# Blocks of w1 and w2 prepared in the f steps instead of in the second product, and the last group of the first product's output taken in another order

## Chip, core and metric

The kernel runs on one core of one Trainium2 chip. The metric is the device time of one execution in microseconds (us). Three runs of the kernel before lie between 1381.03 and 1382.69 us, with a median of 1381.96 us.

## The reference

Attention in two steps feeds two gated products one after the other. All inputs are float32 (the weights arrive as 64-bit words and are converted in the kernel).

```python
p_packed = sm_attn(p, k, v)              # 8 batches, 8 heads, 32 packed queries, head size 64
out = sm_attn(q, p_packed, p_packed)     # 576 tokens per batch
x = out as (4608 tokens, 512)
# first MoE
g = x @ w_gate;  val = x @ w_val         # 512 -> 1536
x = (silu(g) * val) @ w_out              # 1536 -> 512
# second MoE
a = x @ w1;  b = x @ w2                  # 512 -> 1024
h = a * b @ w3                           # 1024 -> 1024
return h @ w_out2                        # 1024 -> 512
```

## The kernel before

Every float32 product is made of three TensorE matmuls: each operand is split into a high part (a cast on ScalarE) and a low part (a subtraction on VectorE or GpSimd), and high times high, high times low and low times high are summed in PSUM. In tile names the last letter tells the part: `uh` and `ul`, `woh` and `wol`, `w3h` and `w3l`.

Engines are PE (TensorE), DVE (VectorE), ACT (ScalarE), POOL (GpSimd) and SP (SyncE, which issues the DMAs). Each engine runs its own instructions in order. The order in the f steps is set when the program is built, by a scheduler with its own estimates, so an edit in one place can move instructions in another. In stage 5 the order is that of the code.

After the attention the first MoE runs in four passes P = 0 to 3, of two batches (1152 tokens) each. A pass has twelve f steps, one for each 128 columns of w_gate and w_val:

- `c_mm` and `c_out`: the packed attention times the weights gives PSUM tile `pc`; ACT makes `ch` of it, DVE `cl`.
- `stage1`: for each of the two batches, twelve matmuls into `pg`, twelve into `pv`. ACT puts the silu of `pg` into `u`, DVE multiplies `u` by `pv`, ACT makes `uh`, POOL `ul`.
- `stage3`: each three f steps make a group. In the first f step after it, six tiles `px` (j = 0 to 5) of 18 matmuls each (three f values, n = 0 to 2, times three parts, times two halves) take up the group; ACT or DVE adds a tile to its accumulator `acc`. The last group, of f = 9, 10, 11 of pass 3, has no f step after it and runs at the end.

`pc`, `pg`, `pv`, `px` and `pw` share four PSUM tiles: a new one starts only when what reads the old one in its place is done.

In passes 1 and 2 there is room beside the f steps, and blocks of w1 and w2 are converted there (`w12_conv`): a block is loaded as 64-bit words into a `raw` tile, a shift on DVE (`vx`), an activation on ACT and a merge on DVE make float32 of it, and it goes to DRAM (`w12d`). In pass 3 the product w3 times w_out2 is made beside the f steps (`w3_task`): w3 is converted (`vx_w`, `vt_w`), transposed on DVE (`w3T`, one buffer), split by ACT and POOL (`w3h`, `w3l`), multiplied into `pw`, and DVE or ACT writes `w3o`, for the second half (`c` = 1) by adding `pw` to `part`, which is the first half's result read back from DRAM.

Stage 5 makes a and b of the second MoE with seven products in place of eight, on sums of 256-wide blocks of w1, w2 and of x. For each of six groups g of tokens and eight steps f it runs seven products of six matmuls (`pA`, `pB`, `pC`). The seven weight blocks of a step are the tiles `ws`. Group g = 0 makes them: `load_w12` reads w12d back, `ws_sums` makes four sums on DVE, `ws_block` splits each of the seven and stores them to DRAM (`wsd`). Groups 1 to 5 load them from there (`ws_load`). Stage 7 (`po`) multiplies a times b with the product of w3 and w_out2 and writes the output.

Of the kernel before, what the change touches and what calls it, by code (L numbers as in the profile page):

```python
# [38 lines left out]
def packed_attention_moe_kernel(  # L39
# [255 lines left out]
    def raw_src(key):  # L295
        what, *at = key.split("_")
        at = [int(x) for x in at]
        if what == "wo2":
            c, kk = divmod(at[0], NH)
            return w_out2[512 * c:512 * c + 512, :].rearrange("(i k a) n -> k i a n", k=NH, a=32)[kk]  # L300
        if what == "w3":
            c, r = at
            return w3[128 * r:128 * r + 128, 512 * c:512 * c + 512].rearrange(
                "(b rr) (i n) -> i b rr n", rr=4, i=4)
        if what == "w":
            return (w_gate, w_val)[at[1]][:, 128 * at[0]:128 * at[0] + 128].rearrange(
                "(k p) n -> p k n", p=128)
        if what == "wo":
            return w_out[128 * at[0]:128 * at[0] + 128, :]
        x, c, h = w12_list[at[0]]  # L310
        return (w1, w2)[x][128 * c:128 * c + 128, 512 * h:512 * h + 512]

    raw_at = [0]
    load_after = {}
# [2 lines left out]
    def raw_load():  # L317
        if raw_at[0] < len(raw_q):
            key = raw_q[raw_at[0]]
            src = raw_src(key)  # L320
            raw_at[0] += 1
            blocks = src.shape[0] == 4
            t = vc.tile([128, 512] if blocks else [128] + list(src.shape[1:]), I64, tag="raw",
                        name=f"raw_{key}", bufs=5)
            if blocks:
# [5 lines left out]
            raw_t.append((key, t))  # L331

    def conv(key, t):

# [322 lines left out]

    CW = 2 * S // 3

    def stage3(P, g, e):  # L660
        for j in range(ND // 2 * 3 // 2 * e, ND // 2 * 3 // 2 * (e + 1)):
            t = psum(f"px{P}_{g}_{j}")
            for n in range(GF):
                f = GF * g + n
                uh, ul = (x.rearrange("p b a s -> p (b a s)") for x in u_pair[P, f])
                wh, wl = wo_t[P, f]
                for w, x, first, last in (
                    (wh, uh, n == 0, False), (wh, ul, False, False), (wl, uh, False, n == GF - 1),
                ):
                    for h in range(2):  # L670
                        d, c = divmod(2 * j + h, 3)
                        nc.tensor.matmul(  # L672
                            t[:, h, 0:CW], lhsT=w[:, 128 * d:128 * d + 128], rhs=x[:, CW * c:CW * c + CW],
                            start=first, stop=last,
                        )
            if g == 0:
                o = up.tile([128, 2, CW], F32, tag=f"acc{j}", name=f"acc{P}_{j}", bufs=1)
                nc.scalar.copy(o, t[:, :, 0:CW])
                acc[j] = o
            else:  # L680
                o = acc[j]
                nc.vector.tensor_tensor(out=o, in0=o, in1=t[:, :, 0:CW], op=ALU.add)  # L682
            if g == NG - 1:
                for h in range(2):
                    d, c = divmod(2 * j + h, 3)
                    t0 = 2 * S * P + CW * c
                    if j % 3 == 1:
                        nc.sync.dma_start(X2d[d, :, t0:t0 + CW], o[:, h])
                    elif h == 0:
                        nc.sync.dma_start(X2d[d, :, t0:t0 + 2 * CW], o.rearrange("p h s -> p (h s)"))  # L690


    def w12_conv(i):
        x, c, h = w12_list[i]
        t = vl.tile([128, 512], F32, tag="vu", name=f"w12t{i}")
        conv(f"w12_{i}", t)
        nc.sync.dma_start(
            w12d[4 * h:4 * h + 4, :, x, c, :].rearrange("f p n -> p f n"),
            t.rearrange("p (f n) -> p f n", n=128))


    wo2_t, w3T = {}, {}
# [42 lines left out]
    def w3_step(new, old):  # L745
        if old is not None:
            w3_mm(old)
        if new is not None:
# [8 lines left out]
    x2_t, x2r_t, w12r_t, wsrc, ws_t, wg_at = {}, {}, {}, {}, {}, []  # L757

    def load_w12(f):
        t = xp.tile([128, 2, 2, 256], F32, tag="wf", name=f"w12r{f}")  # L760
        nc.sync.dma_start(t.rearrange("p x k n -> p x (k n)"), w12d[f].rearrange("p x c n -> p x (c n)"))
        w12r_t[f] = t

    def ws_sums(f):
        t = w12r_t.pop(f)
        a11, a12, a21, a22 = (t[:, x, kh] for x in range(2) for kh in range(2))
        sa = vl.tile([128, 2, 256], F32, tag="vu", name=f"wsa{f}")
        sb = vl.tile([128, 2, 256], F32, tag="vu", name=f"wsb{f}")
        tt = nc.vector.tensor_tensor
        tt(out=sa[:, 0], in0=a21, in1=a22, op=ALU.add)  # L770
        tt(out=sa[:, 1], in0=sa[:, 0], in1=a11, op=ALU.subtract)
        tt(out=sb[:, 0], in0=a11, in1=a21, op=ALU.subtract)
        tt(out=sb[:, 1], in0=a12, in1=sa[:, 1], op=ALU.subtract)
        wsrc[f] = {"A11": a11, "A12": a12, "A22": a22, "S1": sa[:, 0], "S2": sa[:, 1],
                   "S3": sb[:, 0], "S4": sb[:, 1]}

    def ws_tile(g, f, k):
        if f == 0:
# [78 lines left out]
    for n, (P, f) in enumerate(steps):  # L857
# [39 lines left out]
        if P == 0:  # L897
# [2 lines left out]
            wo_split(P, f)  # L900
            if n >= 2:
                pin.clear()
        i = n - NF - 3
        if 0 <= i < len(w12_list):
            pin.update(pin_at)
            w12_conv(i)
            pin.clear()
        if P + 1 < NPR:
            q_tasks(2 * P + 2, 0, f)
            q_tasks(2 * P + 3, 5, f)  # L910
        if pend is not None:
            stage3(*pend, 1)
            pend = None
        C_t.pop((P, f))
        if f % GF == GF - 1:
            pend = (P, f // GF)
        if P == NPR - 1:
# [13 lines left out]
                x2_prep(0, 2)  # L931
            if f == 11:
                x2_prep(0, 3)
                load_w12(0)
                ws_sums(0)
                for k in range(7):
                    ws_block(0, k)
    for e in range(2):
        stage3(*pend, e)
        if e == 0:  # L940
            load_w12(1)
            ws_sums(1)
            load_w12(2)
    up.release()
    aB.release()
    wop.release()
# [24 lines left out]
    def stage5(g, f):  # L971
# [3 lines left out]
        def product(k, first):  # L975
            n, _, name = PROD[k]
            xh, xl = x2_t[g, name]
            w = ws_t[f, k]
            for d in range(2):
                for i, (hl, r) in enumerate(((0, xh), (0, xl), (1, xh))):  # L980
                    nc.tensor.matmul(bk[n], lhsT=w[:, hl, 128 * d:128 * d + 128], rhs=r[:, d],  # L981
                                     start=(first and d == 0 and i == 0), stop=(d == 1 and i == 2),
                                     skip_group_check=not first)

        def ahead(k):

            if g == 0 and f + 1 < NF2:
                ws_block(f + 1, k)
            n = (NF2 - 1) * g + f + 1
            ng, nf = divmod(n, NF2 - 1)  # L990
            if f and 0 < ng < NG2:
                ws_load(ng, nf + 1, k)

        def keep(name, t):
# [113 lines left out]
```

## Time and profile before

| | before |
|---|---|
| median of 3 runs | 1381.96 us |
| profiled execution | 1378.52 us |
| its span, first to last instruction | 1376.7 us |
| mean granted TensorE clock in it | 0.995 |
| PE busy | 1344.1 us (98%) |
| DVE busy | 658.7 us (48%) |
| ACT busy | 572.3 us (42%) |
| POOL busy | 386.0 us (28%) |
| DMA queue, share of its 16 engines' span | 53.8%, 228.64 MB |

The profile is of one execution, 3.4 us shorter than the median run; 1.8 us of that execution lie outside the span. Busy matmuls are counted from start to modelled end, so time in which TensorE runs at the lower clock counts as busy too.

### The profile page before, as it was taken

The page shows a single profiled execution, that of the slowest core. Times are in us where ns is not written, and L with a number is a line of the kernel's source. Part 1 is how long each engine was busy: PE and PEld are TensorE (multiplying, and loading weights), DVE is VectorE, ACT ScalarE, POOL GpSimd, SP SyncE. Part 2 cuts the span into 40 slices and gives each one's busy share as a digit, 9 for nine tenths or more (in the row PEclk, how much of TensorE's full clock was granted, in tenths as well). Part 3 has the DMA queues.
Part 4 walks back from the last instruction along what each step waited for, and adds up shares of the span by engine and source line. Part 5 has one row for each costly group of instructions (what it writes and reads, how often), then busy time and mean ns, then how long its engine had stood idle before and what let it go on. Part 6 is the DMA issues. An engine that isn't in the chain of part 4 may idle for free.

```text
span 1376.7 us, 25585 instructions
## 1 busy us (share of the span) xinstructions
PE 1344.1 (98%) x10196; PEld 1235.3 (90%) x10196; DVE 658.7 (48%) x962; ACT 572.3 (42%) x956; POOL 386.0 (28%) x309
## 2 busy tenths in 40 slices
PE   6889999999999999999999999999999999999998
PEld 4669899999999999999898989989899899898997
DVE  2875867346563466462354378733413333234230
ACT  4784644235432444344544136433323233233231
POOL 0323322323322233253443226502112022021120
PEclk9999999999999999999999999999999999999999
DMA  9997766534455444145343238928548367285441
GB/s 281 314 268 212 228 188 200 153 97 133 125 127 181 124 135 123 55 144 148 120 130 104 82 121 308 347 70 254 173 131 254 105 198 231 74 253 170 132 152 46
DMA packets 195335, 230.28 MB, mean 167 GB/s; under 512 B 71056, under 2 KB 128400, under 8 KB 195216
## 3 DMA queue, kind: packets, MB, share of 16 engines
q1 hardware_dynamic: 195216, 228.64, 53.8%
q8 instruction: 81, 1.33, 0.4%
q14 instruction: 38, 0.31, 0.1%
HBM read 179.04 MB, written 49.55 MB: 166 GB/s over the span
## 4 chain that ended last, share of the span: by engine, by line
PE 85%; POOL 1%; DVE 1%; ACT 1%; issue 0%; DVEq 0%; POOLq 0%; ACTq 0%
PE px L672 20%; PE pA L981 15%; PE po L1045 14%; PE pg L441 10%; PE pv L441 9%; PE pB L981 7%; PE pC L981 4%; PE pc L409 3%; PE pw L736 3%; PE psq L206 1%; POOL wo2l L89 0%; POOL ul L89 0%; DVE u L450 0%; DVE xB21l L89 0%; ACT vt_wo L346 0%
## 5 line engine op out<-in xcount | busy, mean ns | idle before, releaser
L89 POOL TENSOR_TENSOR ul<-u,uh 128x576 fp32r<-128x576 f32 x96 | 146.7, 1528 | 329.3 <-ACT uh L93 324.2
L1001 POOL TENSOR_TENSOR c<-s,s 128x384 f32<-128x384 f32 x48 | 49.2, 1024 | 375.7 <-ACT s L996 375.5
L672 PE MATMUL px<-uh,woh 128*128 128x384 f32 x576 | 148.0, 337 | 2.4 <-DVE acc L682 1.4
L672 PE MATMUL px<-ul,woh 128*128 128x384 f32 x576 | 147.8, 337 | 2.5 <-POOL ul L89 2.5
L672 PE MATMUL px<-uh,wol 128*128 128x384 f32 x576 | 147.2, 336 | 0.0
L996 ACT COPY s<-pA 128x384 f32<-128x384 f32 x144 | 69.2, 481 | 182.6 <-PE pA L981 181.2
L450 DVE TENSOR_TENSOR u<-u,pv 128x576 f32<-128x576 f32 x96 | 71.8, 749 | 108.1 <-PE pv L441 98.2
L93 ACT CAST uh<-u 128x576 fp32r<-128x576 f32 x96 | 64.6, 673 | 115.1 <-DVE u L450 114.8
L682 DVE TENSOR_TENSOR acc<-acc,px 128x768 f32<-128x768 f32 x72 | 68.1, 948 | 92.4 <-PE px L672 92.2
L1045 PE MATMUL po<-wo_hi,abl 128*128 128x512 f32 x288 | 112.2, 390 | 0.0
L1045 PE MATMUL po<-wo_lo,abh 128*128 128x512 f32 x288 | 112.2, 389 | 0.0
L1045 PE MATMUL po<-wo_hi,abh 128*128 128x512 f32 x288 | 112.0, 389 | 0.0
L672 PEld LDWEIGHTS px<-uh,woh 128*128 128x128 f32 x576 | 103.5, 189 | 5.3 <-DVE acc L682 1.9
L672 PEld LDWEIGHTS px<-ul,woh 128*128 128x128 f32 x576 | 104.8, 189 | 3.1 <-POOL ul L89 3.1
L672 PEld LDWEIGHTS px<-uh,wol 128*128 128x128 f32 x576 | 104.9, 189 | 0.0
L89 DVE TENSOR_TENSOR abl<-ab,abh 128x768 fp32r<-128x768 f32 x48 | 48.6, 1013 | 105.1 <-ACT abh L93 105.1
L89 POOL TENSOR_TENSOR wol<-wof,woh 128x512 fp32r<-128x512 f32 x48 | 63.2, 1330 | 108.2 <-ACT woh L93 105.5
L441 PE MATMUL pg<-aTh,ch 128*128 128x288 f32 x384 | 87.2, 308 | 2.1 <-ACT u L446 1.2
L446 ACT ACTIVATE u<-pg 128x576 f32<-128x576 f32 x96 | 62.5, 651 | 60.6 <-PE pg L441 59.1
L441 PE MATMUL pv<-aTh,ch 128*128 128x288 f32 x384 | 82.9, 297 | 0.9 <-DVE cl L89 0.6
L441 PE MATMUL pg<-aTh,cl 128*128 128x288 f32 x384 | 82.3, 296 | 0.0
L441 PE MATMUL pv<-aTh,cl 128*128 128x288 f32 x384 | 82.2, 295 | 0.0
(309 smaller groups left out, 3099.0 us busy)
## 6 DMA issues: line engine op xcount, KB each, us to landing
ws<-wsd SPq DMA_DIRECT2D x245, 256.0 KB, 3.1
wf<-Wd SPq DMA_DIRECT2D x36, 512.0 KB, 4.8
wsd<-ws SPq DMA_DIRECT2D x49, 256.0 KB, 3.1
wof<-wod SPq DMA_DIRECT2D x36, 256.0 KB, 3.0
x2r<-X2d SPq DMA_DIRECT2D x24, 384.0 KB, 4.7
out_dram<-o SPq DMA_DIRECT2D x36, 256.0 KB, 2.0
km<-in_k_dram SPq DMA_DIRECT2D x16, 512.0 KB, 6.9
vm<-in_v_dram SPq DMA_DIRECT2D x16, 512.0 KB, 7.9
```

The source lines that it names most:

```text
L89: return eng.tensor_tensor(out=out, in0=src, in1=hi.bitcast(F32), op=ALU.subtract)
L93: nc.scalar.copy(hi, src)
L409: nc.tensor.matmul(t[hs[at], b, Q], lhsT=PTd[es, 2 * (2 * P + b) + Q, hs[hq]], rhs=w[es, 2 * Q + hq // 2].rearrange("p g n -> p (g n)"), s ...
L441: nc.tensor.matmul(t[:, hf, 0:HS], lhsT=w[:, b % 2, Q, cols], rhs=x[:, Q, hf, :], start=first, stop=last,)
L446: x = nc.scalar.activation(u, t[:, :, 0:HS], AF.Silu)
L450: x = nc.vector.tensor_tensor(out=u, in0=u, in1=t[:, :, 0:HS], op=ALU.mult)
L672: nc.tensor.matmul(t[:, h, 0:CW], lhsT=w[:, 128 * d:128 * d + 128], rhs=x[:, CW * c:CW * c + CW], start=first, stop=last,)
L682: nc.vector.tensor_tensor(out=o, in0=o, in1=t[:, :, 0:CW], op=ALU.add)
L981: nc.tensor.matmul(bk[n], lhsT=w[:, hl, 128 * d:128 * d + 128], rhs=r[:, d], start=(first and d == 0 and i == 0), stop=(d == 1 and i == 2) ...
L996: nc.scalar.copy(o, t)
L1001: on.tensor_tensor(out=r, in0=o, in1=t, op=op)
L1045: nc.tensor.matmul(t, lhsT=a[:, j, cols], rhs=w[:, f], start=first, stop=last)
```

## The change

- A block is now a pair (f, d): the four 128x128 pieces that step f of stage 5 needs from 128 rows of both halves of w1 and w2. They are loaded by four DMAs into one raw tile.
- Blocks are converted two at a time in every third f step of passes 1 and 2 (the steps that also run `stage3`), eight steps with two blocks each. There the four sums are made (DVE), all seven pieces are split (ACT with DVE, and ACT with POOL) and stored to `wsd`. `w12d`, `load_w12`, `ws_sums` and `ws_block` go.
- Group 0 of stage 5 loads its `ws` from `wsd` as the others do. A block in `wsd` has another layout: a load takes pieces of 1 KB where it took 2 KB.
- Raw loads are filled up to five in flight, or two while blocks of w1, w2 or w_out2 are next; before, each conversion issued one load.
- The last `px` group: for tiles 0 to 3 the matmuls of n = 0 and 1 (f = 9 and 10) come first, then n = 2 tile by tile.

The core of the diff:

```diff
-    w12_list = [(x, c, h) for h in range(2) for x in range(2) for c in range(ND)]
+    w12_list = [(f, d) for f in range(NF2) for d in range(2)]
...
+    def raw_fill():
+        if w12_at[0] == len(w12_list):
+            depth = 5
+        else:
+            depth = 2 if raw_q[raw_at[0]].startswith(("w12", "wo2")) else 5
+        while raw_at[0] < len(raw_q) and len(raw_t) < depth:
+            raw_load()
...
-        if not in_front[0]:
-            raw_load()
+        if not in_front[0] and not key.startswith("w12"):
+            raw_fill()
...
+    def stage3_last(P, g):
+        ahead = {j: psum(f"px{P}_{g}_{j}") for j in range(4)}
+        for j in ahead:
+            stage3_mm(P, g, j, ahead[j], range(GF - 1))
+        for j in range(ND // 2 * 3):
+            t = ahead.get(j) or psum(f"px{P}_{g}_{j}")
+            stage3_mm(P, g, j, t, range(GF - 1 if j in ahead else 0, GF))
+            stage3_out(P, g, j, t)
...
+    def w12_blocks(i):
+        f, d = w12_list[i]
+        t = w12_t.pop(i).rearrange("p (k n) -> p k n", k=4)
+        a11, a12, a22, a21 = (t[:, k] for k in range(4))
+        x = vc.tile([128, 512], I32, tag="vx", name=f"w12s{i}").bitcast(F32).rearrange("p (k n) -> p k n", k=4)
+        s1, s2, s3, s4 = (x[:, k] for k in range(4))
+        tt = nc.vector.tensor_tensor
+        tt(out=s1, in0=a21, in1=a22, op=ALU.add)
+        tt(out=s2, in0=s1, in1=a11, op=ALU.subtract)
+        tt(out=s3, in0=a11, in1=a21, op=ALU.subtract)
+        tt(out=s4, in0=a12, in1=s2, op=ALU.subtract)
+        for src, k0, k1, on in ((t[:, 0:3], 0, 3, "dve"), (x, 3, 7, "pool")):
+            o = vc.tile([128, k1 - k0, 2, 128], F32R, tag="raw", name=f"w12p{i}_{k0}", bufs=5)
+            split(o[:, :, 0], o[:, :, 1], src, sub_on=on)
+            w12_out.append((wsd[f, d, :, k0:k1], o))
+        w12_at[0] += 1
...
     def ws_load(g, f, k):
         t = ws_tile(g, f, k)
-        nc.sync.dma_start(t.bitcast(F32).rearrange("p h (d n) -> p h d n", d=2), wsd[f, k])
+        nc.sync.dma_start(t.bitcast(F32), wsd[f, :, :, WSK[k]].rearrange("d p h n -> p d (h n)"))
...
-        i = n - NF - 3
-        if 0 <= i < len(w12_list):
+        w12_new = range(2 * (n - NF) // 3, 2 * (n - NF) // 3 + 2) if 0 < P < NPR - 1 and f % GF == 0 else ()
+        if w12_new:
             pin.update(pin_at)
-            w12_conv(i)
+            for i in w12_new:
+                w12_conv(i)
             pin.clear()
+            for i in w12_new:
+                w12_blocks(i)
...
-                load_w12(0)
-                ws_sums(0)
                 for k in range(7):
-                    ws_block(0, k)
-    for e in range(2):
-        stage3(*pend, e)
-        if e == 0:
-            load_w12(1)
-            ws_sums(1)
-            load_w12(2)
+                    ws_load(0, 0, k)
+    stage3_last(*pend)
...
-            if g == 0 and f + 1 < NF2:
-                ws_block(f + 1, k)
             n = (NF2 - 1) * g + f + 1
             ng, nf = divmod(n, NF2 - 1)
-            if f and 0 < ng < NG2:
+            if (f or g == 0) and ng < NG2:
                 ws_load(ng, nf + 1, k)
```

The matmuls are the same before and after. The change moves instructions on the in-order engines, and three places show it. In these rows the number behind a name and an underscore is a batch in pairs, an f, a tile or a buffer: `u_8` is the u of f = 8, `px_3_1` tile 1 of group 3, `w3o_0` the first output of the second half of w3, `w_1_6` the seventh block of that half.

First, VectorE in pass 3, f = 7 to 8. Before:

```order
573 L450 TENSOR_TENSOR u_7_8474<-u_7_8474,pv_7_8489 128x576
574 L450 TENSOR_TENSOR u_7_8527<-u_7_8527,pv_7_8542 128x576
575 L742 TENSOR_TENSOR w3o_0_8573<-part_8559,pw_1_0_8558 128x512
576 L719 STREAM_TRANSPOSE w3T(1, 3)_8737<-vt_w_1_3_8678 128x512
577 L350 SCALAR_TENSOR_TENSOR vt_w_1_5_8776<-vt_w_1_5_8776,vx_w_1_5_8777 128x512
578 L347 TENSOR_SCALAR vx_w_1_7_8951<-raw_w_1_7_8683 128x512
579 L89 TENSOR_TENSOR cl_9_8614<-pc_9_8596,ch_9_8613 128x1024
580 L450 TENSOR_TENSOR u_8_8617<-u_8_8617,pv_8_8632 128x576
581 L742 TENSOR_TENSOR w3o_1_8669<-part_8655,pw_1_1_8654 128x512
582 L719 STREAM_TRANSPOSE w3T(1, 4)_8770<-vt_w_1_4_8743 128x512
```

Now, from the w3T(1, 4) of the same f step on (L771 is the transpose, L794 the write of w3o):

```order
656 L771 STREAM_TRANSPOSE w3T(1, 4)_9009<-vt_w_1_4_8982 128x512
657 L364 SCALAR_TENSOR_TENSOR vt_w_1_5_9015<-vt_w_1_5_9015,vx_w_1_5_9016 128x512
658 L464 TENSOR_TENSOR u_8_8927<-u_8_8927,pv_8_8942 128x576
659 L771 STREAM_TRANSPOSE w3T(1, 5)_9094<-vt_w_1_5_9015 128x512
660 L361 TENSOR_SCALAR vx_w_1_6_9101<-raw_w_1_6_8766 128x512
661 L364 SCALAR_TENSOR_TENSOR vt_w_1_6_9100<-vt_w_1_6_9100,vx_w_1_6_9101 128x512
662 L794 TENSOR_TENSOR w3o_0_8817<-part_8803,pw_1_0_8802 128x512
663 L771 STREAM_TRANSPOSE w3T(1, 6)_9183<-vt_w_1_6_9100 128x512
664 L89 TENSOR_TENSOR cl_10_9038<-pc_10_9020,ch_10_9037 128x1024
665 L361 TENSOR_SCALAR vx_w_1_7_9190<-raw_w_1_7_8831 128x512
666 L364 SCALAR_TENSOR_TENSOR vt_w_1_7_9189<-vt_w_1_7_9189,vx_w_1_7_9190 128x512
667 L464 TENSOR_TENSOR u_9_9041<-u_9_9041,pv_9_9056 128x576
```

w3o_0 stood right behind the second u of f = 7 and ahead of w3T(1, 3); it now stands behind w3T(1, 5) and the merge of vt_w_1_6. w3o_1 to w3o_3, which before were spread over f = 8, now come behind the u of f = 9. TensorE's order here is unchanged: pw_1_0, pc_9, the pg and pv of f = 8 with pw_1_1 and pw_1_2 between them, pw_1_3, pc_10, pg and pv of f = 9, pw_1_4, px_2_0. In the built program pw_1_0 to pw_1_3 lie in the four PSUM tiles, pc_10 waits for w3o_0, pg_9 for cl_10, pv_9 for the silu on ACT, pw_1_4 for u_9; each follows the other in one PSUM tile.

The DMA queue of SyncE at the same place, now (before, the loads of raw_w_1_7 stood ahead of the store of w3o_0, L743):

```order
297 L332 DMA raw_w_1_6_8766<-in_moe_w_dram 32x4x128 x4
298 L783 DMA part_8803<-wo3d 128x512
299 L332 DMA raw_w_1_7_8831<-in_moe_w_dram 32x4x128 x2
300 L795 DMA wo3d<-w3o_0_8817 128x512
301 L332 DMA raw_w_1_7_8831<-in_moe_w_dram 32x4x128 x2
302 L388 DMA wf_11_8894<-Wd 128x1024
303 L403 DMA wof_9_8896<-wod 128x512
```

Two of the four loads of raw_w_1_7 now stand behind the store of w3o_0, and on ACT the conversion of w_1_7 stands ahead of the silu of f = 9.

Second, TensorE in the last px group. Before, the first tile is finished before the second begins:

```order
2355 L672 MATMUL px_3_0_9322<-uh_9_8831,woh_9_8748 128x384 x2
2356 L672 MATMUL px_3_0_9322<-ul_9_8832,woh_9_8748 128x384 x2
2357 L672 MATMUL px_3_0_9322<-uh_9_8831,wol_9_8749 128x384 x2
2358 L672 MATMUL px_3_0_9322<-uh_10_9153,woh_10_9099 128x384 x2
2359 L672 MATMUL px_3_0_9322<-ul_10_9154,woh_10_9099 128x384 x2
2360 L672 MATMUL px_3_0_9322<-uh_10_9153,wol_10_9100 128x384 x2
2361 L672 MATMUL px_3_0_9322<-uh_11_9247,woh_11_9214 128x384 x2
2362 L672 MATMUL px_3_0_9322<-ul_11_9248,woh_11_9214 128x384 x2
2363 L672 MATMUL px_3_0_9322<-uh_11_9247,wol_11_9215 128x384 x2
```

Now, at the end of the matmuls that do not need f = 11:

```order
2378 L684 MATMUL px_3_3_9549<-ul_9_9071,woh_9_8987 128x384 x2
2379 L684 MATMUL px_3_3_9549<-uh_9_9070,wol_9_8988 128x384 x2
2380 L684 MATMUL px_3_3_9549<-uh_10_9392,woh_10_9338 128x384 x2
2381 L684 MATMUL px_3_3_9549<-ul_10_9393,woh_10_9338 128x384 x2
2382 L684 MATMUL px_3_3_9549<-uh_10_9392,wol_10_9339 128x384 x2
2383 L684 MATMUL px_3_0_9546<-uh_11_9486,woh_11_9453 128x384 x2
2384 L684 MATMUL px_3_0_9546<-ul_11_9487,woh_11_9453 128x384 x2
```

The first matmul that reads uh_11 was the 13th of the group and is now the 49th.

Third, VectorE in pass 0, f = 2, where q of the next batch is transposed in two instructions for the product psq. Before:

```order
160 L157 STREAM_TRANSPOSE qT_0_1836<-qr_0_1762 128x576
161 L450 TENSOR_TENSOR u_2_1869<-u_2_1869,pv_2_1884 128x576
162 L157 STREAM_TRANSPOSE qT_0_1836<-qr_0_1762 128x576
163 L350 SCALAR_TENSOR_TENSOR wf_4_1903<-wf_4_1903,vx_w_1_1910 128x4x128
164 L347 TENSOR_SCALAR vx_wo_1949<-raw_wo_1755 128x512
165 L450 TENSOR_TENSOR u_2_1917<-u_2_1917,pv_2_1932 128x576
166 L350 SCALAR_TENSOR_TENSOR wof_2_1948<-wof_2_1948,vx_wo_1949 128x512
```

Now:

```order
160 L464 TENSOR_TENSOR u_2_1870<-u_2_1870,pv_2_1885 128x576
161 L364 SCALAR_TENSOR_TENSOR wf_4_1904<-wf_4_1904,vx_w_1_1911 128x4x128
162 L156 STREAM_TRANSPOSE qT_0_1837<-qr_0_1763 128x576
163 L361 TENSOR_SCALAR vx_wo_1950<-raw_wo_1718 128x512
164 L364 SCALAR_TENSOR_TENSOR wof_2_1949<-wof_2_1949,vx_wo_1950 128x512
165 L156 STREAM_TRANSPOSE qT_0_1837<-qr_0_1763 128x576
166 L464 TENSOR_TENSOR u_2_1918<-u_2_1918,pv_2_1933 128x576
```

The second transpose now stands behind the shift and the merge of a block of w_out.

## Rows read from the trace of the kernel before

**Rows 1.** The page, first part: busy time of each engine.
```profile
PE 1344.1 (98%) x10196; PEld 1235.3 (90%) x10196; DVE 658.7 (48%) x962; ACT 572.3 (42%) x956; POOL 386.0 (28%) x309
```
**Rows 2.** Waits of PE: total us, times, longest us.
```profile
PE px L672 <- POOL ul L89: 2.5, 2, 1.5
PE px L672 <- DVE acc L682: 1.4, 1, 1.4
PE px L672 <- ACT uh L93: 1.0, 2, 0.7
```
**Rows 3.** Chain of waits, pass 3: start us, us, what.
```profile
636.32 9.37 PE px L672 x54
```
**Rows 4.** Timeline of PE, last px group: start, us, what, idle before.
```profile
799.88 0.51 PE L672 MATMUL px<-uh,woh 128*128 128x384 f32 x2
...
807.51 0.84 PE L672 MATMUL px<-uh,wol 128*128 128x384 f32 x2
808.15 0.84 PE L672 MATMUL px<-uh,woh 128*128 128x384 f32 x2
...
825.50 0.34 PE L981 MATMUL pA<-xB11h,ws 128*128 128x384 f32 x1
```
**Rows 5.** Windows there: busy PE, PEld, DVE, ACT, POOL; PEclk; DMA.
```profile
805.00:810.00 5.00, 3.53 (x10) 3.13 (x11) 4.52 (x4) 0.00 (x0) 1.98 (x1) 0.51 0.24 71
```
**Rows 6.** Timeline of POOL, last px group.
```profile
802.89 4.09 POOL L89 TENSOR_TENSOR ul<-u,uh 128x576 fp32r<-128x576 f32 x2 [4.00 <-ACT uh L93]
```
**Rows 7.** Timeline of DVE, pass 3, f = 7 to 9.
```profile
732.64 0.69 DVE L742 TENSOR_TENSOR w3o<-part,pw 128x512 f32<-128x512 f32 x1 [1.94 <-PE pw L736]
...
750.01 0.71 DVE L719 STREAM_TRANSPOSE w3T(1, 5)_8855<-vt_w 128x512 f32<-128x512 f32 x1 [3.15 <-POOL w3l(1, 4)_8773 L89]
...
754.78 1.19 DVE L89 TENSOR_TENSOR cl<-pc,ch 128x1024 fp32r<-128x1024 f32 x1
755.89 0.74 DVE L450 TENSOR_TENSOR u<-u,pv 128x576 f32<-128x576 f32 x1
```
**Rows 8.** Timeline of ACT, the same stretch.
```profile
750.76 0.66 ACT L346 ACTIVATE vt_w<-raw_w 128x512 f32<-128x512 f32 x1 [2.75 <-DVE w3T(1, 5)_8855 L719]
751.32 1.15 ACT L93 CAST w3h(1, 5)_8857<-w3T(1, 5)_8855 128x512 fp32r<-128x512 f32 x1
752.38 1.01 ACT L420 CAST ch<-pc 128x1024 fp32r<-128x1024 f32 x1
753.28 0.66 ACT L446 ACTIVATE u<-pg 128x576 f32<-128x576 f32 x1
```
**Rows 9.** Timeline of PE, the same stretch.
```profile
748.38 1.09 PE L409 MATMUL pc<-wf,PTd 64*32 64x256 f32 x32
749.41 0.53 PE L441 MATMUL pg<-aTh,ch 128*128 128x288 f32 x2
...
752.89 0.47 PE L736 MATMUL pw<-wo2h,w3h(1, 4)_8772 128*128 128x512 f32 x1
```
**Rows 10.** DMA issues: count, KB each, median us from issue to landing.
```profile
ws<-wsd SPq DMA_DIRECT2D x245, 256.0 KB, 3.1
raw_w<-in_moe_w_dram SPq DMA_DIRECT2D x16, 512.0 KB, 4.3
raw_w<-in_moe_w_dram SPq DMA_DIRECT2D x64, 128.0 KB, 3.6
raw_w<-in_moe_w_gate_dram SPq DMA_DIRECT2D x12, 512.0 KB, 6.5
```
**Rows 11.** Timeline of DVE, pass 0, f = 2.
```profile
114.53 1.64 DVE L347 TENSOR_SCALAR vx_wo<-raw_wo 128x512 int32<-128x512 int32 x1
```
**Rows 12.** Windows: pass 1; stage 5, g = 0 and g = 1.
```profile
300.00:350.00 50.00, 50.00 (x412) 46.95 (x411) 30.29 (x35) 23.79 (x33) 14.67 (x10) 1.00 0.38 110
825.50:885.50 60.00, 60.00 (x338) 58.32 (x338) 52.60 (x90) 38.65 (x95) 38.58 (x37) 1.00 0.88 316
918.10:976.50 58.40, 58.40 (x338) 58.38 (x337) 18.82 (x30) 20.39 (x40) 15.46 (x16) 1.00 0.67 215
```

More of the change, by code (lines that the diff above doesn't have):

```diff
@@ L309, in raw_src @@
             return w_out[128 * at[0]:128 * at[0] + 128, :]
-        x, c, h = w12_list[at[0]]
-        return (w1, w2)[x][128 * c:128 * c + 128, 512 * h:512 * h + 512]
+        f, d = w12_list[at[0]]
+        return [(w1, w2)[x][128 * (2 * kh + d):128 * (2 * kh + d) + 128, 128 * f:128 * f + 128]
+                for x, kh in ((0, 0), (0, 1), (1, 1), (1, 0))]
     raw_at = [0]
@@ L321, in raw_load @@
             raw_at[0] += 1
-            blocks = src.shape[0] == 4
-            t = vc.tile([128, 512] if blocks else [128] + list(src.shape[1:]), I64, tag="raw",
+            parts = isinstance(src, list)
+            blocks = not parts and src.shape[0] == 4
+            t = vc.tile([128, 512] if blocks or parts else [128] + list(src.shape[1:]), I64, tag="raw",
                         name=f"raw_{key}", bufs=5)
-            if blocks:
+            if parts:
+                for i in range(4):
+                    nc.sync.dma_start(t[:, 128 * i:128 * i + 128], src[i])
+            elif blocks:
                 for i in range(4):
@@ L658, in packed_attention_moe_kernel, with stage3_mm, stage3_out @@
     CW = 2 * S // 3
+    def stage3_mm(P, g, j, t, ns):
+        for n in ns:
+            f = GF * g + n
+            uh, ul = (x.rearrange("p b a s -> p (b a s)") for x in u_pair[P, f])
+            wh, wl = wo_t[P, f]
+            for w, x, first, last in (
+                (wh, uh, n == 0, False), (wh, ul, False, False), (wl, uh, False, n == GF - 1),
+            ):
+                for h in range(2):
+                    d, c = divmod(2 * j + h, 3)
+                    nc.tensor.matmul(
+                        t[:, h, 0:CW], lhsT=w[:, 128 * d:128 * d + 128], rhs=x[:, CW * c:CW * c + CW],
+                        start=first, stop=last,
+                    )
+    def stage3_out(P, g, j, t):
+        if g == 0:
+            o = up.tile([128, 2, CW], F32, tag=f"acc{j}", name=f"acc{P}_{j}", bufs=1)
+            nc.scalar.copy(o, t[:, :, 0:CW])
+            acc[j] = o
+        else:
+            o = acc[j]
+            nc.vector.tensor_tensor(out=o, in0=o, in1=t[:, :, 0:CW], op=ALU.add)
+        if g == NG - 1:
+            for h in range(2):
+                d, c = divmod(2 * j + h, 3)
+                t0 = 2 * S * P + CW * c
+                if j % 3 == 1:
+                    nc.sync.dma_start(X2d[d, :, t0:t0 + CW], o[:, h])
+                elif h == 0:
+                    nc.sync.dma_start(X2d[d, :, t0:t0 + 2 * CW], o.rearrange("p h s -> p (h s)"))
     def stage3(P, g, e):
@@ L662, in stage3 @@
             t = psum(f"px{P}_{g}_{j}")
[L663 to L690, printed above, removed]
+            stage3_mm(P, g, j, t, range(GF))
@@ L702, in packed_attention_moe_kernel, with w12_store @@
+    w12_out = []
+    def w12_store():
+        while w12_out:
+            to, o = w12_out.pop(0)
+            nc.sync.dma_start(to, o.bitcast(F32))
     wo2_t, w3T = {}, {}
@@ L756, in packed_attention_moe_kernel @@
             ("A", "S3", "T3"), ("C", "A12", "B21"), ("A", "A22", "T4"))
[L757 to L775, printed above, removed]
+    WSK = [("A11", "A12", "A22", "S1", "S2", "S3", "S4").index(name) for _, name, _ in PROD]
+    x2_t, x2r_t, ws_t, wg_at = {}, {}, {}, []
     def ws_tile(g, f, k):
@@ L1051, in packed_attention_moe_kernel @@
     load_wo3(0)
+    for k in range(7):
+        ws_load(0, 1, k)
     with tc.manual_schedule(engines=M0):
```

26 lines of the change are left out of this document (10 added, 16 removed).

## The prediction

> **What bounds the kernel now.** I read the busy times first. PE is busy for 98% of the span, DVE for 48%, ACT for 42%, POOL for 28% [rows 1]. The matmuls stay the same, so the change can only move the time in which PE waits or runs at its lower clock. It can save little and can cost much: any new wait shows in full.
>
> So the waits of PE came next. Inside the f steps the list is short: px waits 2.5 us for POOL's ul in two places, 1.0 us for ACT's uh in two places and 1.4 us once for DVE's acc [rows 2]. The timeline puts the ul and uh waits into the last px group. It lasts from 799.88 to 825.50, which is 25.62 us for 108 matmuls [rows 4]. A px half group of 54 matmuls takes 9.37 us in the chain of waits [rows 3], so 108 should take 18.74. The last group loses 6.9 us: 3.5 in waits [rows 2], the other 3.4 because PE then runs at the lower of its two levels, 1.2 GHz. The granted clock of the window 805 to 810 is 0.51 [rows 5], and a pair of matmuls takes 0.64 us (from 807.51 to 808.15) [rows 4] where full speed gives 2 x 9.37 / 54 = 0.35.
>
> **The last group.** The late values are those of f = 11: POOL makes the last two ul from 802.89 to 806.98 [rows 6]. Before, the 13th matmul already reads f = 11. After, 48 matmuls that need only f = 9 and 10 come first, and they last 48 x 9.37 / 54 = 8.3 us, so f = 11 is first read at about 799.9 + 8.3 = 808.2, 1.2 us after ul is there. The four px tiles take the four PSUM tiles; the reads that free these are the last u, done by 802.9, where ACT's uh and POOL follow. Gain 6.9 us. Were ul over 1.2 us later than now, some of the wait and perhaps the low clock would stay: bounds 4 and 6.9.
>
> **Group 0 of stage 5.** The windows give 60.0 us to g = 0 and 58.4 to g = 1, with PE full in both [rows 12], for the same matmuls up to the first po. DVE's 52.6 us and POOL's 38.6 us in g = 0 are near g = 1's 18.8 and 15.5 once blocks come ready made [rows 12]. I take the whole difference, 1.5 us (bounds 0 and 1.6).
>
> **The acc wait of 1.4 us** [rows 2] lies at pass 3, f = 0: an acc stood behind a w3T that waited for POOL. In the new order of DVE it no longer does. Gain 1.4 us (bounds 0 and 1.4).
>
> **Blocks in the f steps of passes 1 and 2.** Two blocks add, at a step, two shifts, two merges, eight sums and two subtractions on DVE. Priced as if each were a whole 128x512 operation at 0.69 us [rows 7] that is 9.7 us; with eight sums of a quarter width, I estimate 5. ACT adds two activations of 0.66 and four casts of up to 1.15 [rows 8], at most 5.9 us. This comes once in three f steps, where the window from 300 to 350 shows PE full, DVE at 30.3 of 50 and ACT at 23.8 [rows 12], part of which is the old conversion. Cover: in those steps PE runs 18.7 us of px, in which each tile of 3.1 us frees a PSUM tile and PE has three others. I cost it at nothing. Were the cover gone, a burst longer than it would put off the next u and so the next pg; I bound that by 2 us a step, 16 us in all.
>
> **The transpose in pass 0, f = 2.** The second half of qT, for psq, now stands behind a shift and a merge. The shift took 1.64 us here [rows 11]; with a merge like the 0.69 us of a DVE operation of that size [rows 7] the transpose is 2.3 us later, and psq, the next product on PE, has almost no slack. Loss 2.0 us (bounds 0 and 2.7).
>
> **The write of w3o in pass 3.** This is the term that decides. Four PSUM tiles hold pw_1_0 to pw_1_3 when PE comes to pc_10. Before, w3o_0 was written at 732.64 [rows 7], long ahead of pc_10, which ran at 748.38 [rows 9]. Now w3o_0 is behind w3T(1, 5), which ran at 750.01 and ended at 750.7, having waited 3.15 us for POOL [rows 7]. That wait is POOL's and ACT's chain for w3l(1, 4), which the change leaves in its order. From there, with durations of before:
>
> - w3h(1, 5) on ACT 1.15, then the activation of w_1_6 0.66 [rows 8], the merge and w3o_0 0.69 each (the size of [rows 7]): w3o_0 is done at 750.7 + 3.2 = 753.9.
> - pc_10 takes 1.03 (748.38 to 749.41) [rows 9], ch 1.01 [rows 8], cl 1.19 [rows 7]: pg_9 starts at 757.1. PE idles 5.5 us ahead of pc_10 and 2.2 behind it.
> - pg and pv took 3.48 us together (749.41 to 752.89) [rows 9], so pg ends at 758.8. The silu takes 0.66 [rows 8], but ACT first converts w_1_7, two of whose loads stand behind the store of w3o_0. A load of 128 KB lands 3.6 us after its issue [rows 10], so near 758; with the conversion's 0.66 the silu starts at about 759 and ends at 759.7.
> - pv ends at 761.4, the u of f = 9 on DVE takes 0.74 [rows 7], and pw_1_4 starts at 762.2. Before, it started at 752.89 [rows 9].
>
> The loss is 9.3 us. It can be smaller where POOL's chain runs earlier without w3o in DVE's way, but w3h(1, 5) needs the buffer that pw_1_3 reads until 748.4 [rows 9], so w3o_0 can't be done before 748.4 + 3.2 = 751.6, 2.3 us sooner: bounds 7 and, with later loads, 11. All of it is on PE's path, as PE does nothing else there. Behind it, w3o_1 to w3o_3 free the px tiles in time, as each tile lasts 3.1 us.
>
> **The clock there.** In this stretch PE works some 4.5 us out of 14. In the last group 3.5 us of waits sufficed for a stretch at half clock that cost 3.4 us. Here at most pc, pg, pv and the next pw, some 7 us, could be doubled, and at least nothing. I take 2.0, below the 3.4, since fewer matmuls run in it. The Trainium skill, TensorE: Matmul & The Clock Gate, Part 1, says the same of the cause: the throttled state is the default, and activity releases it; by that a stretch this idle should show the low level. The trace agrees for the last group (0.51).
>
> **DMA.** A ws load goes from 2 KB to 1 KB pieces. A load of 256 KB lands in 3.1 us now [rows 10]; stage 5 loads 7 each f step, 7.3 us, and the share of g = 1 is 0.67 [rows 12]. The nearest rows on piece size are the 512 KB loads: 4.3 us in 4 KB rows (w3 blocks), 6.5 in 1 KB rows [rows 10], a factor of 1.5, which bounds the cost from above; nothing from below. I take a tenth, which stays hidden. The Trainium skill, DMA: Bandwidth & Descriptors, Why small descriptors are slow, gives a fixed cost of some three cycles a packet beside 32-byte beats; my estimate from it is 35 against 67 beats for half the bytes, 4 to 5% more. No run here shows that rule yet.
>
> **Sum.** -6.9 - 1.5 - 1.4 + 2.0 + 9.3 + 2.0 = +3.5 us. The profiled execution took 1378.5 us (span 1376.7 and 1.8 around it), so 1382.0 in its terms. The median is 3.4 us above that execution; I move it by the same sum: 1382.0 + 3.5 = 1385.5 us. A difference under 0.2%, 2.8 us, is about what a measurement of this kernel can't tell from none.
>
> **The rivals.**
>
> - *There is no stall.* In the built program pc_10 waits for a count of DVE's instructions; I read it as w3o_0's. Were it an earlier one, such as the u of f = 8, pc_10 would run on time and gains of 9.8 and a loss of 2.0 leave -7.8: 1374 us, faster. It decides at 748.4: whatever pc_10 waits for must be done by then. For it: PE's order is unchanged, and PE didn't wait here before. Against it: nothing else than w3o_0 reads pw_1_0, and four tiles are full. Chance 0.18.
> - *The f steps of passes 1 and 2 leak.* Eight steps at up to 2 us, on top of the forecast: 1390 to 1401. For it: DVE's share there is 60%. Against: the px cover. Chance 0.12.
> - *DMA becomes the bound in stage 5.* With the factor 1.5, the share of 0.67 in g = 1 comes to 1.0, and denser stretches exceed it: some 0.2 of 7.3 us lost in each of 30 to 40 f steps, 45 us or more, 1430. Against: PE was full at a share of 0.88 in g = 0 [rows 12]. Chance 0.04.
> - *Nothing comes of it*: the new waits are hidden and the old ones come back in other places, 1382. Chance 0.05.
>
> The forecast has 0.61. Its own range is 1379 to 1391: the stall 7 to 11, the clock 0 to 7, the last group 4 to 6.9, qT 0 to 2.7. It ends above 1384.7 in about 0.36 of the 0.61, within 0.2% in 0.22, faster in 0.03. With the rivals: faster 0.03 + 0.18 = 0.21, same 0.22 + 0.05 = 0.27, slower 0.36 + 0.12 + 0.04 = 0.52. For 8 in 10 the range reaches down to the first rival and a little into the second: 1373 to 1393.
>
> **What would show it.** The last px group near 18.7 us, at full clock, with no wait for ul. In pass 3, PE idle about 5 us ahead of a pc that waits for DVE's w3o, then shorter waits of pg for cl, pv for ACT, pw for u, and a window with a low clock. A wait of psq for qT in pass 0. g = 0 of stage 5 at 58.4 us, DMA share below 1. PE full in passes 1 and 2. The prediction is wrong if the pc has no such wait, or if PE waits for ws in stage 5.

## The result and the profile after

The changed kernel takes 1392.42 us, the median of four runs (1389.62 to 1394.68); the kernel before took 1381.49 in the same comparison. The ratio is 1.0079 with a 95% interval of 1.0054 to 1.0103: slower, by 10.9 us. The forecast was slower by 3.5 us, 1385.5, in a range of 1373 to 1393. The direction was right; the size was a third of what came, and the time lies at the upper edge of the range.

The profiled execution took 1394.68 us, the longest of the four, with a span of 1392.9 against 1376.7. The tally below is of these two profiles, so it explains 16.2 us, not 10.9. Busy time of each engine:

```profile
PE 1352.6 (97%) x10196; PEld 1242.4 (89%) x10196; DVE 650.3 (47%) x978; ACT 569.1 (41%) x932; POOL 379.0 (27%) x301
```

DVE, ACT and POOL have less to do than in [rows 1] and the matmuls are as many, yet PE shows 8.5 us more busy time: it ran longer at its lower clock (mean granted clock 0.988, before 0.995). The waits of PE in the list of all waits (total us, times, longest):

```profile
PE pc L423 <- DVE w3o L794: 5.2, 1, 5.2
PE pv L455 <- ACT u L460: 5.0, 4, 1.8
PE pg L455 <- DVE cl L89: 3.3, 2, 2.4
PE pg L455 <- ACT u L460: 1.6, 2, 1.1
PE psq L205 <- DVE qT L156: 1.4, 1, 1.4
PE pw L788 <- DVE u L464: 0.9, 1, 0.9
```

Against [rows 2], no px waits any more. In their place stand a pc that waits for w3o, and pg and pv that wait for the silu u and for cl. PE's timeline shows the stall in pass 3 and the two ends of the last px group:

```profile
762.12 1.96 PE L423 MATMUL pc<-wf,PTd 64*32 64x256 f32 x32 [5.17 <-DVE w3o L794]
766.51 0.85 PE L455 MATMUL pg<-aTh,ch 128*128 128x288 f32 x2 [2.42 <-DVE cl L89]
770.50 0.85 PE L455 MATMUL pv<-aTh,ch 128*128 128x288 f32 x2 [0.74 <-ACT u L460]
774.66 0.80 PE L788 MATMUL pw<-wo2h,w3h(1, 4)_9011 128*128 128x512 f32 x1 [0.92 <-DVE u L464]
...
823.80 0.51 PE L684 MATMUL px<-uh,woh 128*128 128x384 f32 x2
...
842.52 0.34 PE L1008 MATMUL pA<-xB11h,ws 128*128 128x384 f32 x1
```

The four waits, for w3o, cl, the silu and u, are those of the prediction, in its order, and come to 9.25 us. The pc takes 1.96 us where [rows 9] has 1.09: it runs at half clock. The windows show for how long (busy PE, PEld, DVE, ACT, POOL; PEclk; DMA share, GB/s):

```profile
760.00:765.00 5.00, 1.96 (x32) 0.68 (x32) 2.69 (x3) 0.81 (x1) 0.93 (x1) 0.71 0.31 95
765.00:770.00 5.00, 3.25 (x12) 2.90 (x12) 2.34 (x3) 1.08 (x3) 0.00 (x0) 0.50 0.95 318
770.00:775.00 5.00, 3.58 (x13) 3.24 (x14) 1.15 (x2) 1.31 (x3) 1.28 (x1) 0.50 0.33 111
775.00:780.00 5.00, 5.00 (x15) 3.96 (x15) 0.89 (x2) 0.70 (x2) 1.42 (x1) 0.58 0.72 208
762.00:779.00 17.00, 12.79 (x66) 9.96 (x67) 5.07 (x8) 3.52 (x5) 2.70 (x2) 0.50 0.63 201
```

By how much later the same group of matmuls starts after than before, the 16.2 us come together so: up to the end of pass 0 +2.5; passes 1 and 2 +10.5 (from +2.55 at 264 us to +13.07 at 574); pass 3 ahead of the stall -4.6; the stall +15.4 (from +8.5 to +23.9); the last group -6.9; group 0 of stage 5 -0.5; the rest of stage 5 -0.3.

Two stretches at the lower clock are in these sums that no wait of the prediction explains, each some 1.6 us by the starts of the matmuls: one behind 93 us, early in pass 0 (granted clock 0.81 and 0.85 in the windows 90 to 95 and 95 to 100, before 1.00), and one in pass 2, behind a wait of 1.83 us:

```profile
465.00:470.00 5.00, 5.00 (x60) 3.81 (x60) 2.53 (x5) 1.90 (x3) 1.68 (x2) 0.66 0.20 66
```

They come and go between executions. The run depth2 below, whose engines work in the same order up to there, has 1.00 in both places and takes 9.8 us more than before in passes 1 and 2, not 10.5.

These 10 us of passes 1 and 2, which the prediction had at nothing, are the surprise. SyncE, pass 1, at the conversion of f = 3:

```profile
313.08 4.78 SPq L751 DMA_DIRECT2D wsd<-w12p  x4
317.91 4.24 SPq L328 DMA_DIRECT2D raw_w<-in_moe_w_dram  x8
322.25 0.38 SPq L403 DMA_DIRECT2D wof<-wod  x1
```

And ACT, a little later:

```profile
325.34 0.65 ACT L460 ACTIVATE u<-pg 128x576 f32<-128x576 f32 x1
328.96 0.62 ACT L93 CAST woh<-wof 128x512 fp32r<-128x512 f32 x1 [2.97 <-DMA wof<-wod]
329.49 0.65 ACT L460 ACTIVATE u<-pg 128x576 f32<-128x576 f32 x1
```

Four stores, the last of which waits for POOL, and eight loads of the next blocks stand ahead of one load of w_out's block (wof). It is issued at 322.25. ACT comes to its cast, woh, at 325.99, finds the load not landed and stands until 328.96. All that is behind it on ACT comes late, up to a silu that ends at 335.1, for which PE waits:

```profile
335.14 0.53 PE L455 MATMUL pv<-aTh,ch 128*128 128x288 f32 x2 [1.57 <-ACT u L460]
```

### The profile page after: what moved, and what is told of

It is laid out like the page before. It is cut to its first block, busy times and chain, and to the rows that moved or that the text cites. A ratio compares the mean times of both kernels' runs of the same rounds, so it can differ in the third digit from the quotient of the medians.

```text
span 1392.9 us, 25689 instructions
## 1 busy us (share of the span) xinstructions
PE 1352.6 (97%) x10196; PEld 1242.4 (89%) x10196; DVE 650.3 (47%) x978; ACT 569.1 (41%) x932; POOL 379.0 (27%) x301
## 4 chain that ended last, share of the span: by engine, by line
PE 80%; issue 3%; DVE 2%; DMA 2%; SPq 2%; POOL 1%; ACT 1%; DVEq 0%; POOLq 0%; ACTq 0%
PE px L684 17%; PE pA L1008 14%; PE po L1070 14%; PE pg L455 9%; PE pv L455 9%; PE pB L1008 7%; PE pC L1008 4%; PE pw L788 3%; PE pc L423 2%; DMA wof<-wod 2%; SPq L328 1%; PE psq L205 1%; POOL ul L89 1%; DMA raw_w<-in_moe_w_dram 0%; ACT u L460 0%
## 5 line engine op out<-in xcount | busy, mean ns | idle before, releaser
L455 PEld LDWEIGHTS pg<-aTh,ch 128*128 128x128 f32 x384 | 62.4, 191 | 25.3 <-issue 10.7
L89 DVE TENSOR_TENSOR cl<-pc,ch 128x1024 fp32r<-128x1024 f32 x48 | 58.3, 1215 | 57.0 <-ACT ch L434 57.0
```

Source lines behind the costliest of these rows:

```text
L89: return eng.tensor_tensor(out=out, in0=src, in1=hi.bitcast(F32), op=ALU.subtract)
L455: nc.tensor.matmul(t[:, hf, 0:HS], lhsT=w[:, b % 2, Q, cols], rhs=x[:, Q, hf, :], start=first, stop=last,)
```

## The experiments

The runs were taken in two rounds on two chips, and each ratio is against the kernel before in its own round: a median of 1381.19 us for the last group alone, two raw loads, wof ahead and the three together, and 1380.41 us for four raw loads, the old order and the blocks behind the softmax.

**The last group alone.** The kernel before, with the new order of the last px group:

```diff
+    def stage3_last(P, g):
...
+            if j == 2:
+                load_w12(1)
+                ws_sums(1)
+                load_w12(2)
...
-    for e in range(2):
-        stage3(*pend, e)
-        if e == 0:
-            load_w12(1)
-            ws_sums(1)
-            load_w12(2)
+    stage3_last(*pend)
```

The loads and sums of the weight blocks stay where they were, behind the third tile.

> The kernel before with one part of the change alone: the last px group in the new order, nothing else. My theory: the wait for POOL's ul and the stretch at half clock behind it were worth 6.9 us, so this kernel takes 1381.5 - 6.9 = 1374.6 us, its last group lasts 18.7 us in place of 25.6, and PE has no wait there. Rival: the wait only moves to the third or fourth px tile, whose PSUM tile is freed by the last u; then 2 to 4 us are left, some at half clock, and the gain is 3 to 5 us.

Measured: 1381.13 us against 1381.19, a ratio of 0.9992 (0.9978 to 1.0005). No gain; my theory falls for this kernel, and the rival too. PE and DVE there:

```profile
816.29 0.62 PE L670 MATMUL px<-uh,woh 128*128 128x384 f32 x2 [3.99 <-DVE acc L682]
```

```profile
811.00 0.43 DVE L788 TENSOR_TENSOR wsa<-w12r 128x256 f32<-128x256 f32 x1 [2.51 <-DMA w12r<-w12d]
...
814.43 0.94 DVE L89 TENSOR_TENSOR ws<-w12r,ws 128x256 fp32r<-128x256 f32 x1
815.29 1.81 DVE L682 TENSOR_TENSOR acc<-acc,px 128x768 f32<-128x768 f32 x2
```

The waits for ul are gone. But now four px tiles are finished late and close together, and the fifth needs one back. DVE's acc, which would free it, stands behind eight sums and splits for the weight blocks, and the first of these waits 2.51 us for a DMA. Behind the wait the clock falls too (0.75 in the window 815 to 820), and the group lasts 24.6 us in place of 25.6, not 18.7. The first pA still starts 1.3 us sooner (824.21 against 825.50), and that is lost again by g = 1 of stage 5, in part where the first po waits 1.1 us for ACT. The new order needs a DVE that is free just then.

**Two raw loads in pass 3.** The changed kernel with

```diff
         if w12_at[0] == len(w12_list):
-            depth = 5
+            depth = 2
```

> The changed kernel with one number changed: in pass 3 two raw loads are kept in flight in place of five. In the built order w3o_0 then stands right behind the second u of f = 7 again, ahead of w3T(1, 3). My theory: the place of w3o_0 on VectorE made the stall of 15.4 us at pc_10 (9.3 us of waits, 6.1 of half clock). Without it the time is 1392.4 - 15.4 = 1377 us, and pc_10 has no wait for w3o. Rival: the chain of w3T, w3h and w3l is late by itself, whatever the place of w3o_0; then PE waits at pc_10 or at the next pw for 3 us or more, and the gain is under 8 us.

Measured: 1378.18 us, 14.2 less than the changed kernel's median; 0.9973 (0.9960 to 0.9987) of the kernel before. PE there:

```profile
755.65 1.09 PE L423 MATMUL pc<-wf,PTd 64*32 64x256 f32 x32
756.67 0.53 PE L455 MATMUL pg<-aTh,ch 128*128 128x288 f32 x2
```

The theory holds: no wait at pc, full clock, and in the profile all of the stall is gone (from pc to the end of pw_1_4 PE loses 0.3 us against the kernel before, where the changed kernel lost 15.4). The depth of the raw loads had moved w3o_0. It moves other instructions of pass 3 as well; that w3o_0's place is what counts rests on PE's wait, which names it, and on the next run.

**Four raw loads in pass 3**, a dose between the two (depth = 4).

> The changed kernel with four raw loads in flight in pass 3, in place of five (or two, in depth2). In the built order w3o_0 stands behind the second u of f = 8, ahead of w3T(1, 5), so pc_10 should not wait for it; but the cast ch stands behind w3h(1, 5) on ACT, and pg, pv and pw of f = 9 still follow pc_10 in one PSUM tile. My theory: PE's loss there is set by the in-order place of each of these on DVE and ACT. With durations of before, w3h(1, 5) ends at 751.9, ch at 752.9, cl at 754.1, so pg waits 4.7 us and pv and pw about 1 us more: some 5.5 us of waits, 3.8 less than with five loads, and the half clock behind them costs in proportion (6.1 us for 9.3), some 3.6: 1378.2 + 9 = 1387 us. Rival on the clock: waits this short don't bring it down, 1378.2 + 5.5 = 1384. Rival on the place: the depth counts by the late loads themselves, and pc_10 still waits for w3o.

Measured: 1382.66 us, 1.0020 (1.0008 to 1.0031) of the kernel before, 4.5 above depth2 (5.3, each taken against the kernel before in its round); against depth2's profile the stretch costs 5.5. The forecast of 1387 is missed by 4. PE and the window:

```profile
761.28 0.54 PE L455 MATMUL pg<-aTh,ch 128*128 128x288 f32 x2 [3.37 <-DVE cl L89]
```

```profile
760.00:765.00 5.00, 3.72 (x19) 3.46 (x20) 3.11 (x4) 1.80 (x3) 2.37 (x2) 0.78 0.42 121
```

As forecast pc does not wait and pg waits for cl, 3.4 us in place of 4.7. The clock falls here too. Of the 5.5 us, 3.4 are this wait and 0.7 a wait of px for w3o; some 1.4 are left for the lower clock, neither nothing nor in proportion to the 6.1 for 9.3. So the place of each instruction on DVE and ACT sets the stall, and the rival on the place, by which pc would still wait for w3o, is out.

**wof ahead of the loads of the blocks.** The changed kernel with

```diff
             wo_load(*at(1))
+        if 0 < P < NPR - 1 and f % GF == GF - 1:
+            raw_fill()
...
         if w12_new:
             w12_store()
-            raw_fill()
```

> The changed kernel with one thing moved: the eight DMAs that load the next two blocks of w1 and w2 are issued two f steps later, behind the load of w_out's block (wof) that the next group's first step needs. Conversion, sums, splits and stores stay as they are. My theory: in passes 1 and 2 PE lost 10.5 us because SyncE issued wof behind these loads and the stores ahead of them, ACT's cast of wof stood waiting, and the silu behind it on ACT came late. Then the time is 1392.4 - 10.5 = 1382 us, with no wait for that silu in passes 1 and 2. Rival: the burst of sums, merges and subtractions on VectorE and ScalarE makes the stall; then the waits stay and the time is within 2 us of 1392.

Measured: 1388.39 us, 1.0051 (1.0034 to 1.0068) of the kernel before: 4.0 less than the changed kernel, not 10.5. SyncE and ACT at the same place:

```profile
318.92 0.32 SPq L403 DMA_DIRECT2D wof<-wod  x1
319.29 3.77 SPq L328 DMA_DIRECT2D raw_w<-in_moe_w_dram  x8
```

```profile
324.03 0.63 ACT L93 CAST woh<-wof 128x512 fp32r<-128x512 f32 x1
```

wof is issued 3.3 us sooner, the cast does not wait, and PE's wait there is gone. ACT's order moved with it: the cast now stands ahead of both silus of that step. Step by step through the starts of PE's groups, 7.7 us of delay go in passes 1 and 2 (1.6 of them the stretch at the lower clock behind 465 us), two delays of 1.1 and 1.0 us, where PE waits for cl, stay, and a new one of 2.6 us, most of it a wait for the silu, comes at the end of pass 2. So the queue, with the place of the cast behind it, is the larger cause and the burst on DVE a smaller one; both theories were too simple.

**The three together.**

```diff
-            depth = 5
+            depth = 2
         else:
-            depth = 2 if raw_q[raw_at[0]].startswith(("w12", "wo2")) else 5
+            depth = 2 if raw_q[raw_at[0]].startswith(("w12", "wo2")) else 4
```

and the move of `raw_fill` above.

> The changed kernel with both of these (two raw loads in flight in pass 3, the loads of w1 and w2 behind wof) and a third: in pass 0 four raw loads in flight in place of five, by which both transposes of q stand ahead of the shift of w_out's block on VectorE again, as in the kernel before. My theory: the three stalls are separate and add up: 1392.4 - 15.4 - 10.5 - 2.5 = 1364 us, 17 below the kernel before, of which 6.9 come from the last group, about 4 from pass 3 at f = 0 and f = 5, and the rest from group 0 of stage 5 and waits that I have not named. Rival: a stall taken away in one place comes back at the next, as PE reaches later work sooner; then the gains add up to less than 20 of the 28 us, 1372 or more.

Measured: 1373.10 us, 0.9936 (0.9913 to 0.9960) of the kernel before. 19.3 us of the expected 28 came, which is the rival's case: a stall came back elsewhere. The stall in pass 3 and the wait of psq are gone. By the profiles, 5.2 us of the 10.5 in passes 1 and 2 are left, as in wof_first, and to be rid of the wait of psq gives 1.4 in place of 2.5, since the changed kernel wins 1.1 us back at waits later in pass 0, which three has as the kernel before has them. Most of the rest lies in what the forecast started from: stalls read in the longest run were taken off the median, 2.3 us below it. The chain of waits at the wait that came new:

```profile
575.57 1.30 POOL wol L89
...
576.89 4.69 DMA wof<-wod
...
582.12 0.65 ACT u L460
```

Here SyncE was free in time, but wof needs the buffer that POOL's wol reads, and wol is late.

**The old order of the last group, in three.**

```diff
-    stage3_last(*pend)
+    for e in range(2):
+        stage3(*pend, e)
```

> The kernel of the run three with the last px group in the old order (all of a tile's three f values before the next tile); in the built program only these matmuls differ, the order of every other engine is the same. The last group alone gave nothing on the kernel before, where two px tiles then waited 5.4 us for DVE's acc behind the sums for the weight blocks. My theory now: the new order saves the 6.9 us only where DVE is free to add up px at once, which the removed block work gives it; and the removed work alone does not bring ul earlier, since the u of f = 11 stands behind the sums and splits of x, which stay. Then this kernel is 6.9 us slower than three: 1373.1 + 6.9 = 1380.0, with the waits for ul as before. Rival: the block work was what made ul late, and the order is of no use; then the time is within 1.5 us of 1373.1.

Measured: 1379.94 us, 6.8 above three, 0.9997 (0.9986 to 1.0008) of the kernel before. The waits of PE are those of [rows 2] again:

```profile
PE px L684 <- POOL ul L89: 2.5, 2, 1.5
PE px L684 <- ACT uh L93: 1.0, 2, 0.7
```

The medians are of two rounds; in the profiles the last group lasts 25.65 us here and 18.73 in three, so the 6.9 us are there. With last_group this shows that they belong to two parts of the change together: neither the new order (1.1 us in the group, nothing in the end) nor the removed block work gives them alone. One reading in the expectation was wrong: of the 5.4 us of waits for acc in last_group, 4.0 are the px wait shown above; the other 1.4 is the acc wait of [rows 2], in pass 3 at f = 0.

**Blocks behind the softmax, in three.**

```diff
             pin.clear()
-            for i in w12_new:
-                w12_blocks(i)
...
         if w12_new:
+            for i in w12_new:
+                w12_blocks(i)
             w12_store()
```

> The kernel of the run three with the sums, splits and stores of the blocks of w1 and w2 written behind the softmax tasks and the second half of px in their f step, where they stood ahead of them. In three four waits of 0.8 to 1.8 us are left in passes 1 and 2, 4.4 us together: two where the softmax on DVE, and cl behind it, come late, two where POOL's wol and with it the load of wof comes late. My theory: the sums and subtractions on DVE and POOL hold these up, so in a place behind them the waits shrink, by 2 to 4 us: 1370 us. Rival: the work is only moved on to the next in-order instruction, as the engines' load in these steps is the same, and the time stays within 1 us of 1373.

(This kernel also fills the raw loads at the end of the last step of pass 2; no run has that alone.) Measured: 1370.63 us, 0.9931 (0.9913 to 0.9948) of the kernel before, from four runs, and the lowest median here. Three has 0.9936 (0.9913 to 0.9960) in the other round, so the times do not tell the two apart; in the profiles this kernel loses 2.9 us in passes 1 and 2, where three loses 5.2. The two waits behind POOL's wol are gone. Those for cl grew, from 1.7 us in three:

```profile
PE pv L455 <- DVE cl L89: 3.1, 3, 1.3
```

The time came out as the theory said, but not by its mechanism. POOL's wol and the load of wof come no sooner: at the first of the two places SyncE issues wof 2.5 us behind the start of pc (533.27 and 530.74), in three 1.5 us (531.93 and 530.47), and ACT's cast waits 3.8 us for it, in three 3.5. PE no longer waits there because its pv does not follow the silu behind that cast any more: it starts at 536.67, the silu at 537.26. At the second place ACT's order changed. In three:

```profile
581.60 0.62 ACT L93 CAST woh<-wof 128x512 fp32r<-128x512 f32 x1 [4.31 <-DMA wof<-wod]
582.12 0.65 ACT L460 ACTIVATE u<-pg 128x576 f32<-128x576 f32 x1
```

Here the silu stands ahead of the cast, and the cast's wait for wof costs PE nothing:

```profile
577.25 0.65 ACT L460 ACTIVATE u<-pg 128x576 f32<-128x576 f32 x1 [0.21 <-PE pg L455]
580.74 0.62 ACT L93 CAST woh<-wof 128x512 fp32r<-128x512 f32 x1 [2.85 <-DMA wof<-wod]
```

On DVE the softmax itself and the splits are one load in one order or the other.

## Why the prediction was right in direction and short in size

- **The write of w3o**: right in mechanism and in size. Forecast 9.3 us in four waits; 9.25 in the profile, and depth2 takes the stall away by moving w3o_0. The loads of w_1_7 did come late (ACT waited 2.5 us for them) but cost nothing, as pg at half clock was later still; that the last two waits fit the forecast so closely is in part chance.
- **The clock there**: the step "I take 2.0, below the 3.4, since fewer matmuls run in it" failed in size. The stall cost 15.4 us, 6.1 more than its waits, near the upper bound of 7. The low level lasted from pc to the end of pw_1_4 (0.50 from 762 to 779), past all the waits, so that nearly all the matmuls in it were doubled, not a part of them. The Trainium skill, TensorE: Matmul & The Clock Gate, Part 1, says that "the default state is throttled, and activity releases the throttle". The trace agrees: the clock fell with the first wait (0.71, then 0.50), and came back during pw_1_4 (0.58 from 775 to 780), where PE works without a wait.
- **Blocks in passes 1 and 2**: the step "I cost it at nothing" failed. I had priced DVE and ACT and named the px tiles as cover, but left SyncE's queue out: twelve DMAs ahead of wof, and behind wof an in-order ACT. The leak was the second rival, with 16 us as its bound; 10.5 came (9.8 in depth2), by another way than it named for the larger part (7.7 us by wof_first, half clock included; most of the rest by the burst).
- **The last group**: 18.72 us (823.80 to 842.52), 6.9 saved, as forecast, with no wait. What the step left out is its condition, a DVE free for acc. In depth2, where the first pA waits 1.0 us for an acc, 5.7 us come.
- **The acc wait** went, 1.6 us against 1.4. Another 3 us went in pass 3 between f = 5 and 8, for waits that I had not counted.
- **The transpose in pass 0**: psq waits 1.4 us, and the stretch costs 2.5 against 2.0; 1.1 us of that come back behind 157 us, where waits for cl and uh shrink. With four loads in flight there (three) all of it is gone. The +2.5 up to the end of pass 0 is another sum that comes out the same: 0.5 gained ahead of pass 0, 1.6 lost to the lower clock behind 93 us, 2.5 at psq, 1.1 back.
- **Group 0 of stage 5** gained 0.5 us of the 1.5. Its windows after, with g = 1 behind it:

```profile
842.52:901.89 59.37, 59.37 (x338) 59.21 (x337) 24.62 (x38) 24.18 (x47) 15.35 (x16) 1.00 0.96 304
934.55:993.00 58.45, 58.45 (x338) 58.42 (x337) 18.83 (x30) 20.39 (x40) 15.51 (x16) 1.00 0.70 214
```

DVE is light there now, so its load [rows 12] was not the whole reason. PE has no wait in g = 0 and full clock; its matmuls start 0.177 us apart on average where g = 1 has 0.173. That DMA at a share of 0.96 slows them is argued, not shown.
- **DMA**: the rival is out. g = 1 takes 58.45 us against 58.40, and its DMA share goes from 0.67 to 0.70, some 4% more, at the same rate. The Trainium skill, DMA: Bandwidth & Descriptors, Why small descriptors are slow, has the fixed cost a packet from which I had estimated 4 to 5%, and the trace agrees.

Taking these terms with their measured sizes, the sum of +3.5 becomes 3.5 + 10.5 + 4.1 (clock) + 1.0 (group 0) + 0.5 (pass 0) - 3.2 (pass 3) - 0.3 (the rest of stage 5) = 16.1, against the profiles' 16.2. The medians differ by 10.9, since this profile was the slowest run of its kernel and that of before lies below all of its kernel's. The two stretches at the lower clock behind 93 and 465 us, 1.6 us each, are part of it; of the other three runs only the mean granted clock is known, 0.991 to 0.994 against 0.988.

Two more things about the forecast. Its own range, 1379 to 1391, is not what its bounds add up to: all lower ends give 1379, but all upper ends give +13.8, or 1396. And that the time lies inside the stated range is in part luck: two terms of the sum were 10.5 and 4.1 us short, and without the 3.2 us that pass 3 gained unforeseen the median would lie above 1393. The range reached that far only because the second rival, with a chance of 0.12, was counted into it.

## What to carry to other kernels

Work that is moved to "where there is room" is paid for in in-order queues, not in busy shares: follow each DMA that it adds to the load behind it, and from there to what stands behind the instruction that waits for it. A prefetch depth is an edit of the schedule; read in the built order where the instruction that frees a PSUM tile now stands. A gain can need two parts of a change at once, so test parts both alone on the old kernel and taken out of the new one. And when an experiment gives the time that was forecast, look in its trace whether it came by the way that was forecast.

## What the runs showed of the hardware

A wait of 3.4 us in one place (depth4) was followed by a granted clock of 0.78 in that window. Waits of 9.25 us in four pieces went with 17 us at the lower level (0.50 from 762 to 779), through the matmuls between and behind them. The same wait of the same order of instructions in pass 2 was followed by the lower clock in two executions (1.83 us, 0.66 in the window 465 to 470; depth4, 2.2 us, 0.66) and not in a third (depth2, 1.67 us, 1.00). A load of 256 KB landed 6.7 us after its issue behind eight loads of 128 KB (wof in pass 1); the median of all such loads went from 3.0 to 4.6 us with the change. A DVE merge of 128x512 took 1.55 us in the stall of pass 3, where others took 0.68.
